# Reordering the end of the first batch's attention: the fourth pair's queries before the second pair's values, its scores and block sums before transposes back, its exponentials first on ScalarE, and the begun tiles behind the last values

## The chip, the cores and the metric

The kernel runs on one core of a Trainium2 chip. The metric is device time in microseconds (us). A profile also has a span, from the first to the last instruction that it records; it is 1.7 to 2.1 us shorter than the time of the same run. Runs that were timed in rounds were all in the fast state; a kernel that ran only once has the state "unknown", and I use such a run for its trace and not for its time.

All times inside a trace are counted from the start of its span.

## The reference, cut to what matters

```
q, k, v: 4 batches x 8 heads x 768 tokens x 64
local scores of a token: keys within 16 positions; beside them 24 summary scores,
        against the maximum of each block of 32 keys
a     = softmax(local and summary scores together)
attn  = a @ [values, block means of the values]
x     = attn as 3072 x 512
P     = exp(x @ w_gate), then 8 rounds of row and column scaling
out   = sum over 8 experts of P[:, e] * (relu(x @ w1[e]) @ w2[e])
```

The experts are most of the work. They need x, so before the first expert can stream, the first batch has to go through attention, and that start is what the change reorders.

## The kernel before

Heads are taken in pairs, four pairs to a batch, numbered from 0. The first batch is done in two halves of its tokens. For pair i and the first half, these steps run, and each has a letter in the orders below:

| letter | step | engine, line in the profile |
|---|---|---|
| T, Q | transposes of keys, of queries (PSUM) | PE, L300 and L312 |
| S, X | local scores, their exponentials | PE L347, ScalarE (ACT) L490 |
| m, s, e | key maximum of each block, summary scores, their exponentials | VectorE (DVE) L335, PE L452, ACT L472 |
| v, V | block sums of the values, their scaled copy | PE L357, DVE L363 |
| b | masks over the exponentials | DVE L495 and L500 |
| A, n | values times weights, division by the sum | PE L512, DVE L542 and L543 |
| t, x | transposes of the result, their copy to xT | PE L550, copy L207 on ACT or DVE |

The "begun tiles" are twelve single matmuls of the first expert (L211, `hps<-xT,w`), begun while attention still runs: three output tiles, each needing xT of pair 0, 1, 2 and 3 in turn.

```
def block_sums(i):                                   # v: needs the load of the pair's values
    sv = v_x[i % NQ]
    vs = bank("a", "vs")
    ...
        nc.tensor.matmul(vs..., lhsT=m_blk[:, g, :], rhs=sv[:, :, g, 0:D], ...)      # L357

def values_h(i, h):                                  # A
    ...
    av = at["av", i, h] = bank("a", "av")            # one of 3 PSUM banks
    ...

def x_out(eng, i, h=None):                           # x: frees the bank of t
    ...
    copy(eng, xT[:, i % PB, t0:t0 + n], at.pop(("tx", i, h))[:, 0:n])                # L207
```

The three banks tagged "a" are shared by v, A and t. A unit that opens a bank must wait until the unit that had that bank before was read out; which reader it waits for changes with the order, and was read from the semaphores of the built program. A planner puts all units in an order for each engine; for the first batch that order is prescribed:

```
plan.follow("PE",  "T0 F0 Q0 v0 S0 T1 Q1 s0 S1 T2 Q2 s1 A0 S2 v1 T3 A1 Q3 s2 t0 S3 v2 t1 s3 v3 A2 A3 t2 t3")
plan.follow("DVE", "m0 V0 k1 m1 b0 q2 b1 n0 V1 m2 b2 n1 m3 x1 V2 b3 V3 n2 n3 x3")
plan.follow("ACT", "k0 q0 X0 q1 e0 X1 k2 e1 X2 k3 q3 x0 e2 X3 e3 x2")
expert0(0, ...)      # begun tiles: may start once s3 is done ("U["ss", PB-1, 0]")
...
for u in plan.order():      # the list in which instructions are emitted
    u.fn()
```

(F0 in the PE order is a filler at the start and not a begun tile. The calls are shortened: the strings are split and looked up.) Loads of queries, keys and values are issued by GpSimd (POOL), one behind the other on one queue; the fourth pair's values (v3's load) are the last of the first batch.

The softmax here doesn't subtract the row's maximum and nothing guards it: scores larger than these inputs give would overflow.

## Time and profile before

| | before |
|---|---|
| time, median of 3 runs | 667.41 us (667.11 to 668.03) |
| span of the profile, granted clock | 665.94 us, 1.00 |
| TensorE busy | 99% of the span |
| fourth pair's transposes t3 start | 20.65 us |
| first instruction from which both orders are the same to the end (the "join": query transposes of the second half, L312) | 21.41 us |

This is PE's timeline before (columns: start us, duration us, engine, line, operation, output and inputs, shape, count):

```profile
15.57 0.34 PE L550 MATMUL tx<-ident_x,xs 128*128 128x128 f16 x3
15.84 0.39 PE L347 MATMUL sg<-qT,kT 64*128 64x160 bf16 x8
...
20.83 0.65 PE L211 MATMUL hps<-xT,w 128*128 128x384 f16 x3
21.41 0.38 PE L312 MATMUL tkq<-ident,qst 64*64 64x64 bf16 x12
```

The reader is to see the order t0, then S3 at 15.84, and at the other end three begun tiles at 20.83 and the join at 21.41. The join is the place at which to compare kernels: a matmul starts only after those before it, so a difference there is the net effect of everything that the change touched.

### The profile page before, as it was taken

What the parts mean: (1) busy time and instruction counts of PE and PEld (TensorE: products, weight loads), DVE (VectorE), ACT (ScalarE), POOL (GpSimd) and SP (SyncE); (2) the same over time, 40 slices, a digit from 0 to 9 for tenths busy, and PEclk for the clock granted to TensorE, in tenths of its full rate; (3) what the DMA queues carried; (4) which work ended last, traced back from release to release, by engine and by line L of the source; (5) the groups of instructions that cost most, each with busy time, mean ns of one, the idle gap of its engine ahead of it and who ended that gap; (6) DMA issues with size and microseconds to landing.
All of it is one profiled execution on the core that took longest, in us unless ns stands there. A gap on an engine that the chain in (4) does not pass through costs nothing.

```text
span 665.9 us, 13246 instructions
## 1 busy us (share of the span) xinstructions
PE 658.1 (99%) x5132; PEld 434.5 (65%) x5132; DVE 550.3 (83%) x1034; ACT 411.8 (62%) x769; POOL 199.0 (30%) x257
## 2 busy tenths in 40 slices
PE   8999999999999999999999999999999999999997
PEld 4666656555676666666666666666666666666666
DVE  7899977798989887887779877888778877988776
ACT  6677766566875566556665665555655656556652
POOL 8999522100132222212322222213122213222123
PEclk9999999999999999999999999999999999999999
DMA  9999952700763747373754666373838465334656
GB/s 168 183 148 144 136 70 42 127 0 2 134 118 62 123 75 123 66 127 65 110 97 72 119 88 104 64 127 65 127 64 138 69 95 96 64 64 111 155 135 202
DMA packets 112558, 67.89 MB, mean 102 GB/s; under 512 B 77936, under 2 KB 90480, under 8 KB 112496
## 3 DMA queue, kind: packets, MB, share of 16 engines
q0 software_dynamic: 94816, 57.46, 65.3%
q1 hardware_dynamic: 17152, 9.58, 6.2%
q8 instruction: 40, 0.66, 0.4%
q14 instruction: 22, 0.18, 0.1%
q10 hardware_dynamic: 528, 0.02, 0.0%
HBM read 52.45 MB, written 6.29 MB: 88 GB/s over the span
## 4 chain that ended last, share of the span: by engine, by line
PE 93%; DMA 3%; issue 1%; DVE 1%; POOL 0%; ACT 0%; POOLq 0%; DVEq 0%; ACTq 0%
PE yps L815 21%; PE pA L764 21%; PE pY L815 16%; PE pQ L764 10%; PE hps L211 6%; PE yps L216 6%; PE pR L764 5%; DMA out_acc<-y 2%; PE sg L347 1%; PE tkq L303 1%; DMA qst<-in_q_dram 1%; PE vs L357 1%; PE av L435 1%; PE av L512 1%; PE tx L550 1%
## 5 line engine op out<-in xcount | busy, mean ns | idle before, releaser
L815 PEld LDWEIGHTS <-h 128*128 128x128 f16 x2352 | 230.1, 98 | 89.9 <-issue 2.0
L843 POOL DMA_DIRECT2D out_acc<-y x120 | 101.4, 888 | 373.0 <-ACT y L839 107.0
L839 ACT ACTIVATE y<-pY,P_sb 128x256 f32<-128x256 f32 x168 | 80.0, 477 | 126.7 <-PE pY L815 124.0
L830 DVE SCALAR_TENSOR_TENSOR out_acc<-yps,P_sb,out_acc 128x512 f32<-128x512 f32 x128 | 95.3, 745 | 28.0 <-PE yps L815 27.9
L798 DVE TENSOR_TENSOR h<-h 128x1024 f16<-128x1024 f16 x168 | 109.2, 684 | 1.3
L815 PE MATMUL pY<-w,h 128*128 128x256 f16 x672 | 100.3, 273 | 0.6 <-ACT y L839 0.6
L764 PE MATMUL pA<-xT,w 128*128 128x512 f16 x336 | 98.6, 379 | 0.0
L815 PE MATMUL yps<-w2sum,h 128*128 128x256 f16 x672 | 97.9, 273 | 0.0
L815 PE MATMUL yps<-w,h 128*128 128x256 f16 x672 | 93.3, 273 | 0.0
L830 DVE SCALAR_TENSOR_TENSOR out_acc<-pY,P_sb,out_acc 128x512 f32<-128x512 f32 x84 | 62.9, 749 | 29.7 <-PE pY L815 28.1
L764 PEld LDWEIGHTS <-w 128*128 128x128 f16 x672 | 65.8, 98 | 31.3 <-issue 0.2
L764 PEld LDWEIGHTS <-w1sum 128*128 128x128 f16 x504 | 49.3, 98 | 44.6
L786 DVE CUSTOM_DVE_ANT_0 h<-pQ,snap 128x512 f16<-128x512 f32 x84 | 57.7, 686 | 6.5 <-ACT snap L207 3.6
L786 DVE CUSTOM_DVE_ANT_0 h<-pA,snap 128x512 f16<-128x512 f32 x84 | 57.5, 684 | 5.4 <-PE pA L764 5.0
L202 ACT ACTIVATE h<-pA 128x512 f16<-128x512 f32 x84 | 50.6, 603 | 12.1 <-PE pA L764 12.0
L202 ACT ACTIVATE h<-pR 128x512 f16<-128x512 f32 x84 | 50.1, 596 | 8.1 <-PE pR L764 8.1
L815 PE MATMUL pY<-w2sum,h 128*128 128x256 f16 x336 | 50.4, 273 | 0.6 <-ACT y L839 0.5
L207 ACT COPY pR<-pA 128x512 f32<-128x512 f32 x82 | 46.8, 571 | 6.7 <-PE pA L764 5.9
L764 PE MATMUL pA<-xsum,w 128*128 128x512 f16 x168 | 50.0, 379 | 0.0
L764 PE MATMUL pQ<-xsum,w1sum 128*128 128x512 f16 x168 | 50.0, 379 | 0.0
L764 PE MATMUL pR<-xT,w 128*128 128x512 f16 x168 | 50.0, 379 | 0.0
L764 PE MATMUL pQ<-xT,w1sum 128*128 128x512 f16 x168 | 50.0, 379 | 0.0
(150 smaller groups left out, 851.6 us busy)
## 6 DMA issues: line engine op xcount, KB each, us to landing
out_acc<-y POOLq DMA_DIRECT2D x120, 256.0 KB, 3.4
w<-in_moe_w_dram POOLq DMA_DIRECT2D x14, 1024.0 KB, 10.3
out_dram<-out_acc SPq DMA_DIRECT2D x24, 256.0 KB, 2.4
qst<-in_q_dram POOLq DMA_DIRECT2D x32, 96.0 KB, 5.6
vx<-in_v_dram POOLq DMA_DIRECT2D x15, 192.0 KB, 6.4
kst<-in_k_dram POOLq DMA_DIRECT2D x24, 96.0 KB, 5.7
w<-in_moe_w_dram POOLq DMA_DIRECT2D x4, 256.0 KB, 7.0
w<-in_moe_w_dram POOLq DMA_DIRECT2D x2, 512.0 KB, 8.5
```

What stands on the lines that cost most here:

```text
L202: nc.scalar.activation(out=out, in_=in_, func=AF.Relu, bias=0.0, scale=1.0)
L207: (nc.scalar.copy if eng == "ACT" else nc.vector.tensor_copy)(out=out, in_=in_)
L211: nc.tensor.matmul(hp[:, 0:n], lhsT=w1s[e][:, dk, f * 128:(f + 1) * 128], rhs=xT[:, dk, t0:t0 + n], start=(dk == 0), stop=(dk == KD - 1))
L216: nc.tensor.matmul(yp[:, d], lhsT=h[:, f, c * 128:(c + 1) * 128], rhs=w2s[e][:, f, d], start=(f == 0), stop=(f == KF - 1))
L303: nc.tensor.transpose(t[:, g * 128:(g + 1) * 128], st[:, g, :, :].rearrange("p j d -> p (j d)"), ident)
L764: nc.tensor.matmul(dst[:], lhsT=lhsT, rhs=rhs, start=first and k == 0, stop=k == HK - 1, skip_group_check=True)
L786: nc.vector._custom_dve(dve_ops.TENSOR_ADD_SAT, out=ring(e, p, q)[:, q % 2, blk, :], in0=at[src, e, p, q][:], in1=at.pop(("snap", n, e, p, ...
L798: nc.vector.tensor_tensor(out=h[:, :, out_, :], in0=h[:, :, a, :], in1=h[:, :, b, :], op=op)
L815: nc.tensor.matmul(dst[:, d], lhsT=lhsT, rhs=rhs, start=f == 0 and n in (1, 5, 2), stop=f == HF - 1, skip_group_check=True)
L830: nc.vector.scalar_tensor_tensor(out=o, in0=y, scalar=scalar, in1=o, op0=ALU.mult, op1=ALU.add)
L839: nc.scalar.activation(out=at[key][:, d], in_=src, func=AF.Copy, bias=0.0, scale=P_sb[:, t, e:e + 1])
L843: nc.gpsimd.dma_start(out=o, in_=at.pop(("y", e, p, c, key))[:], accum_op=ALU.add)
```

## The change

Its intent is to get the fourth pair's exponentials and masks done earlier, so that the last two values groups follow each other at once, and to let the begun tiles fill the wait behind them. It moves Q3 before A1, S3 before t0 and v3 before t1 on PE; it puts X3 first on ScalarE, with e2 ahead of x0 behind it, and gives the copy x1 from VectorE to ScalarE; and the begun tiles wait for A3.

```diff
-  m = add("PE", 0.165, ..., [xs[dk], w[f // 2], m if dk else U["ss", PB - 1, 0]], ...)
+  m = add("PE", 0.165, ..., [xs[dk], w[f // 2], m if dk else U["A", PB - 1, 0]], ...)
 ...
-  "T0 F0 Q0 v0 S0 T1 Q1 s0 S1 T2 Q2 s1 A0 S2 v1 T3 A1 Q3 s2 t0 S3 v2 t1 s3 v3 A2 A3 t2 t3"     # PE
+  "T0 F0 Q0 v0 S0 T1 Q1 s0 S1 T2 Q2 s1 A0 S2 v1 T3 Q3 A1 s2 S3 t0 v2 v3 t1 s3 A2 A3 t2 t3"
-  "m0 V0 k1 m1 b0 q2 b1 n0 V1 m2 b2 n1 m3 x1 V2 b3 V3 n2 n3 x3"                                # DVE
+  "m0 V0 k1 m1 b0 q2 b1 n0 V1 m2 b2 n1 m3 V2 b3 V3 n2 n3 x3"
-  "k0 q0 X0 q1 e0 X1 k2 e1 X2 k3 q3 x0 e2 X3 e3 x2"                                            # ACT
+  "k0 q0 X0 q1 e0 X1 k2 e1 X2 k3 q3 X3 e2 x0 e3 x1 x2"
```

More of the change, by code (lines that the diff above doesn't have):

```diff
@@ L1000, in expert0 @@
                         m = add("PE", 0.165, lambda f=f, dk=dk: hidden0(key, t0, f, [dk]),
-                                [xs[dk], w[f // 2], m if dk else U["ss", PB - 1, 0]], 9 + f * 0.01,
+                                [xs[dk], w[f // 2], m if dk else U["A", PB - 1, 0]], 9 + f * 0.01,
                                 **{"uses" if dk else "opens": [buf]})
@@ L1075 @@
         plan.follow("PE", [first[c[0]](int(c[1])) for c in
-                           "T0 F0 Q0 v0 S0 T1 Q1 s0 S1 T2 Q2 s1 A0 S2 v1 T3 A1 Q3 s2 t0 S3 v2 t1 s3 v3 A2 A3 t2 t3".split()])
+                           "T0 F0 Q0 v0 S0 T1 Q1 s0 S1 T2 Q2 s1 A0 S2 v1 T3 Q3 A1 s2 S3 t0 v2 v3 t1 s3 A2 A3 t2 t3".split()])
         plan.follow("DVE", [first[c[0]](int(c[1])) for c in
-                            "m0 V0 k1 m1 b0 q2 b1 n0 V1 m2 b2 n1 m3 x1 V2 b3 V3 n2 n3 x3".split()])
+                            "m0 V0 k1 m1 b0 q2 b1 n0 V1 m2 b2 n1 m3 V2 b3 V3 n2 n3 x3".split()])
         plan.follow("ACT", [first[c[0]](int(c[1])) for c in
-                            "k0 q0 X0 q1 e0 X1 k2 e1 X2 k3 q3 x0 e2 X3 e3 x2".split()])
+                            "k0 q0 X0 q1 e0 X1 k2 e1 X2 k3 q3 X3 e2 x0 e3 x1 x2".split()])
         expert0(0, [U["x", i, 0] for i in range(PB)])
```

## The prediction

> **What bounds the kernel now.** I read the page first: the busy row, and the summary of the chain that ended last.
>
> ```profile
> PE 658.1 (99%) x5132; PEld 434.5 (65%) x5132; DVE 550.3 (83%) x1034; ACT 411.8 (62%) x769; POOL 199.0 (30%) x257
> ...
> PE 93%; DMA 3%; issue 1%; DVE 1%; POOL 0%; ACT 0%; POOLq 0%; DVEq 0%; ACTq 0%
> ```
>
> TensorE carries 93% of the chain and its clock row shows full speed in every slice. The instruction order of the two builds gives 10,242 rows on PE in both and no difference after about 21 us: the change adds no work and removes none, it reorders a stretch between 13 and 21 us. So only the empty places of PE in that stretch can be gained. I looked for them next, in PE's timeline (columns: start us, duration us, engine, line, operation). Since the ends are modelled, I take start to next start as what a group occupies.
>
> ```profile
> 16.17 0.52 PE L357 MATMUL vs<-vx,m_blk 128*128 128x128 bf16 x6
> 16.52 0.33 PE L550 MATMUL tx<-ident_x,xs 128*128 128x128 f16 x3
> 16.91 0.34 PE L452 MATMUL ss<-qT,ks 64*32 64x384 bf16 x2
> 17.18 0.52 PE L357 MATMUL vs<-vx,m_blk 128*128 128x128 bf16 x6
> ...
> 18.36 0.66 PE L211 MATMUL hps<-xT,w 128*128 128x384 f16 x3
> 18.86 0.63 PE L512 MATMUL av<-vx,Eh 128*128 128x65 bf16 x16
> ...
> 20.04 0.49 PE L211 MATMUL hps<-xT,w 128*128 128x384 f16 x2
> 20.65 0.34 PE L550 MATMUL tx<-ident_x,xs 128*128 128x128 f16 x3
> ```
>
> Three tx transposes occupy 0.17 us where nothing waits (19.87 to 20.04), but those at 16.52 last until 16.91: 0.22 us empty. Two hps matmuls occupy 0.33 (three take 0.50 at 18.36), but those at 20.04 last until 20.65: 0.28 us empty. The weight loads name the causes:
>
> ```profile
> 16.91 0.09 PEld L452 LDWEIGHTS <-ks 64*32 64x32 bf16 x2 [0.23 <-DVE ks L335]
> ...
> 20.64 0.17 PEld L550 LDWEIGHTS <-xs 128*128 128x128 f16 x3 [0.51 <-DVE xs L543]
> ```
>
> The first waits for the fourth pair's key maximum, the second for the fourth pair's normalized values. Together 0.50 us, 0.07% of 667.41: that is nearly all the change can win here, and no state or clock effect is in play.
>
> **What the Trainium skill says.** "TensorE: Matmul & The Clock Gate", section "The mechanism", says matmuls start and end in strict program order. That is why one late operand holds all behind it; the trace agrees (nothing between 16.69 and 16.91 though other operands were ready). "Perfetto Trace Analysis", section "Tensor Engine Instruction (MATMUL, LD_WEIGHTS)", says the matmul end is an estimate; the trace agrees, groups overlap on paper (16.17 + 0.52 is after 16.52). "ScalarE: Activation LUTs", section "What ACT_TABLE_LOAD costs", gives 186 ns + 0.833 ns per column with immediates, and 93 ns of overlap back to back: 1.01 us for 992 columns, 0.51 for 384. The trace has 0.98 and 0.48, and a spacing of 0.87 and 0.39; I use the trace's.
>
> **The change, part by part.** Letters: Q queries' transposes, S scores, X their exponentials, s/e summaries and their exponentials, v/V block sums and their copy, A values, n normalize, t/x transposes back and their copy, F the begun hidden tiles; the pair's number from 0.
>
> *Q3 ahead of A1.* Twelve transposes of 0.31 us (14.67 to 14.98) swap with A1's 0.84 (13.83 to 14.67). The sum is the same, so s2 still starts at 15.30. Q3's copy on ScalarE can start after the key copy, 14.74, and end near 15.14: in time for S3.
>
> *S3 ahead of t0, X3 first on ScalarE.* S3 starts behind s2 at 15.57 instead of 15.84, its last matmul ends at 15.96. X3 was held by two others:
>
> ```profile
> 15.95 0.48 ACT L207 COPY xT<-tx 128x384 f16<-128x384 f16 x1 [0.38 <-PE tx L550]
> 16.32 0.48 ACT L472 ACTIVATE es<-ss 64x384 bf16<-64x384 f32 x1
> 16.71 0.98 ACT L490 ACTIVATE erh<-sg 128x992 bf16<-128x992 f32 x1
> ```
>
> Now X3 runs 16.01 to 17.00, 0.70 earlier. The price: e2 starts at 16.88 and x0 at 17.27, ending 17.75 instead of 16.43.
>
> *Masks and values.* VectorE does:
>
> ```profile
> 15.91 0.94 DVE L335 TENSOR_REDUCE ks<-kT 128x24 bf16<-128x768 bf16 x1
> 16.89 0.36 DVE L207 COPY xT<-tx 128x384 f16<-128x384 f16 x1
> 17.16 0.28 DVE L363 TENSOR_TENSOR Vs<-vs,own_n 64x128 bf16<-64x128 f32 x1
> 17.72 0.66 DVE L495 TENSOR_TENSOR Eh<-erh,band 128x960 bf16<-128x960 bf16 x1 [0.28 <-ACT erh L490]
> ```
>
> The copy x1 goes to ScalarE, so V2 moves to 16.78-17.06 and the masks of pair 3 to about 17.04-17.77, 0.68 earlier (they ended at 18.45). A3 may then follow A2 directly, without the three F between.
>
> *New waits.* I read from the build which semaphore each PE instruction waits for. v3 now stands before t1, and needs its load and n1 (done 16.00). t1's PSUM slot is v2's, so it waits for V2: 17.06 + 0.04 = 17.10. A2's slot is t0's, so it waits for x0: 17.79. For v3's load I have the queue that waits for its landing:
>
> ```profile
> 16.89 0.75 POOL L190 DMA_DIRECT2D w<-in_moe_w_dram  x1 [1.16 <-DMA vx<-in_v_dram]
> ```
>
> The fourth pair's values landed shortly before 16.89 (the trace's own record: 16.61). So v3 can't start at 16.41, where PE would be ready, but at 16.66 to 16.9.
>
> *The sum.* Occupancies from the timeline: S 0.32, t 0.17 (0.27 before a 64-row group), v 0.35, s 0.27, A 0.84, F 0.165 each. S3 15.57-15.89, t0 to 16.06, v2 to 16.41, **wait 0.25**, v3 16.66-17.01, **wait 0.09**, t1 17.10-17.37, s3 to 17.64, **wait 0.15**, A2 17.79-18.63, A3 to 19.47, two F to 19.80, t2 to 19.97, four F to 20.62, t3 at 20.62. n3 needs A3's end + 0.10 + 0.79 + 0.06 = 20.42, so t3 no longer waits for it: the six F (the same six as before, all ahead of t3) fill that gap. Before, t3 started at 20.65. The two waits of 0.50 us go; three of 0.49 come. **Net gain: 0.03 us**, and about 0.1 at most if v3's load arrives as recorded. Behind t3 both orders are the same, so what is left at t3 stays to the end. PE waits for no load between 21 and 110 us in the view of waits, so an earlier or later PE is not absorbed.
>
> **The rivals.**
> 1. *The intended gain.* A3 ends at 19.45 instead of 19.70, all F fill the wait for n3; if PE did not wait for v3's load and x0, t3 could start 0.3 to 0.45 earlier: 667.0. For it: X3 and the masks really come 0.7 earlier. Against it: the landing at 16.61 and x0 at 17.75 are the new ends of the waits. If ScalarE gets through e2 sooner (it can't start before X3 ends), or the load lands earlier in that run, up to 0.2 of this is won.
> 2. *The wait grows.* v3 stands ahead of t1, s3 and both A in strict order, so a later landing delays them one for one once it exceeds about 16.8. The loads between 5 and 20 us run on DMA engines that are busy in every slice (9 tenths), so a landing moves from run to run; 0.3 later makes 667.6.
> 3. *VectorE or DMA takes the shift back later.* VectorE is busy 7.8 to 9 tenths there, but the loads of the second batch land 2 us and more before PE uses them (the fifth pair's keys by 25.05, used at 27.87), so I see no absorber; this would only pull the result towards 667.4.
>
> **Range and chances.** 667.41 less 0.03, and a little for rival 1, which I hold more likely than rival 2 (the order was written to shorten this stretch): 667.3 us. The three runs before span 667.11 to 668.03, 0.9 us, far more than the effect; a new median of few runs should differ by 0.3 or 0.4 by itself. Add 0.3 for the mechanism: 666.6 to 668.0 holds 8 in 10. A 2% step is 13.3 us, 26 times all the idle time in the stretch: same 0.98, faster 0.01, slower 0.01.
>
> **What would show each step right or wrong.** In the changed profile: S3 at 15.5 to 15.6 and the exponential of 992 columns right behind, near 16.0; the fourth pair's vs group later than the end of the third's, waiting for a vx load or starting at 16.6 to 16.9; the first values after s3 near 17.8, with ScalarE's xT copy ending just before; the two values groups back to back; no wait of a tx weight load for xs near 20.6; the tx of the fourth pair at 20.4 to 20.8. Busy time of all engines unchanged. The prediction is wrong if the tx of the fourth pair starts before 20.2 or after 21.0, or if PE shows a new gap behind 21 us, which I exclude because the order there is the same; and a difference beyond 1 us between fast runs would need a cause that I do not see.

## The result, and the profile after

| | before | after |
|---|---|---|
| median of 5 runs | 667.38 us (667.11 to 668.03) | 667.65 us (667.14 to 668.09) |
| span of the profile | 665.94 us | 665.93 us |
| t3 starts | 20.65 us | 20.96 us |
| join | 21.41 us | 21.71 us |

The ratio is 1.0003, with a 95% interval of 0.9990 to 1.0017: the same. (A ratio is the mean time of one kernel's runs over the mean of the other's in the same rounds, so it is not quite the ratio of the medians.) The busy row and the summary of the chain say nearly the same as before (POOL has the 1% that VectorE had):

```profile
PE 658.9 (99%) x5132; PEld 434.9 (65%) x5132; DVE 550.2 (83%) x1033; ACT 411.7 (62%) x770; POOL 198.8 (30%) x257
...
PE 93%; DMA 3%; POOL 1%; issue 1%; ACT 0%; DVE 0%; POOLq 0%; DVEq 0%; ACTq 0%
```

One instruction has gone from VectorE to ScalarE (1034 to 1033 and 769 to 770: the copy x1), and nothing else was added or removed. This is PE's timeline in the stretch, after:

```profile
15.56 0.39 PE L347 MATMUL sg<-qT,kT 64*128 64x160 bf16 x8
...
16.07 0.51 PE L357 MATMUL vs<-vx,m_blk 128*128 128x128 bf16 x6
17.25 0.50 PE L357 MATMUL vs<-vx,m_blk 128*128 128x128 bf16 x6 [0.68 <-DMA vx<-in_v_dram]
17.59 0.33 PE L550 MATMUL tx<-ident_x,xs 128*128 128x128 f16 x3
...
18.12 0.64 PE L512 MATMUL av<-vx,Eh 128*128 128x65 bf16 x16
...
18.96 0.64 PE L512 MATMUL av<-vx,Eh 128*128 128x65 bf16 x16
...
20.96 0.33 PE L550 MATMUL tx<-ident_x,xs 128*128 128x128 f16 x3
```

The fourth pair's scores are first, at 15.56. The third pair's block sums start at 16.07 and occupy 0.34 us, so PE was ready for the fourth pair's at 16.41. It started them at 17.25. The bracket gives the idle time and its releaser: 0.68 us, until the load of vx landed. (0.68 is counted from the modelled end of the group before; from the next possible start it is 0.84.) From there on nothing waits. The two values groups follow each other (18.12, 18.96), and t3 comes at 20.96.

ScalarE, VectorE and GpSimd in that order show the rest, after:

```profile
16.06 1.00 ACT L490 ACTIVATE erh<-sg 128x992 bf16<-128x992 f32 x1 [0.95 <-ACT qT L207]
...
17.32 0.47 ACT L207 COPY xT<-tx 128x384 f16<-128x384 f16 x1
```

```profile
17.09 0.66 DVE L495 TENSOR_TENSOR Eh<-erh,band 128x960 bf16<-128x960 bf16 x1
```

```profile
17.40 0.74 POOL L190 DMA_DIRECT2D w<-in_moe_w_dram  x1 [1.23 <-DMA vx<-in_v_dram]
```

The exponentials start at 16.06 and the masks at 17.09, where the prediction had 16.01 and 17.04. So the wanted effect came, 0.63 to 0.65 us earlier than before. The copy x0 ends at 17.79. GpSimd, which waits for the same load as PE, is released at 17.40, where it was 16.89 before. The trace's own record has the load landed at 17.11, against 16.61 before.

Two questions follow. Is the late landing the whole of the 0.30 us at the join? And did the new order cause it? A third is why the two profiles have the same span although one is 0.30 us behind at the join.

### The profile page after: what moved, and what is told of

Its sections match the earlier page's. It is cut to its first block, busy times and chain, and to the rows that moved or that the text cites. A ratio compares the mean times of both kernels' runs of the same rounds, so it can differ in the third digit from the quotient of the medians.

```text
span 665.9 us, 13247 instructions
## 1 busy us (share of the span) xinstructions
PE 658.9 (99%) x5132; PEld 434.9 (65%) x5132; DVE 550.2 (83%) x1033; ACT 411.7 (62%) x770; POOL 198.8 (30%) x257
## 4 chain that ended last, share of the span: by engine, by line
PE 93%; DMA 3%; POOL 1%; issue 1%; ACT 0%; DVE 0%; POOLq 0%; DVEq 0%; ACTq 0%
PE yps L815 21%; PE pA L764 21%; PE pY L815 16%; PE pQ L764 10%; PE hps L211 6%; PE yps L216 6%; PE pR L764 5%; DMA out_acc<-y 2%; PE sg L347 1%; DMA vx<-in_v_dram 1%; PE tkq L303 1%; PE vs L357 1%; PE av L512 1%; PE av L435 1%; PE tx L550 1%
## 5 line engine op out<-in xcount | busy, mean ns | idle before, releaser
L764 PE MATMUL pA<-xsum,w1sum 128*128 128x512 f16 x168 | 50.0, 379 | 0.0
```

Source lines behind the costliest of these rows:

```text
L764: nc.tensor.matmul(dst[:], lhsT=lhsT, rhs=rhs, start=first and k == 0, stop=k == HK - 1, skip_group_check=True)
```

## The experiments

**Theory A.** The landing moves from run to run for reasons that are not in the order; the new order exposes it, and the landing at 17.11 is the whole loss. With an early landing, the changed kernel is where the one before is. **Rival B.** Something else, x0 and the bank that it frees or the place of the begun tiles, holds t3 near 20.96 anyway. **Rival C.** The new order makes the load land later. (The expectation of a_again gives the letter C to another rival, that t3 lies anywhere by scatter; t3 3.71 us behind v3 in both late runs speaks against that one.) There was also a constructive question: which parts of the change are worth keeping?

Instead of prescribing another order to the planner, I moved single units in the finished list, which leaves everything behind the join as it was. All edits below use this helper, ahead of the emission, and the data dependencies are asserted again:

```
seq = plan.order()
def behind(after, *us):
    for u in us:
        seq.remove(u); seq.insert(seq.index(after) + 1, u); after = u
...                                                  # the edit of the experiment
assert all(at_[d] < at_[u] for u in seq for d in u.true)
```

### Summary of the traces

Landing is the trace's own record of v3's load. The last column counts from the start of s2 (15.28 to 15.45 in all of them), which removes small shifts that were there before the stretch.

| run | order | v3's load landed | v3 starts | A2 | A3 | t3 | join | join behind s2 |
|---|---|---|---|---|---|---|---|---|
| before | before | 16.61 | 17.18 | 17.53 | 18.86 | 20.65 | 21.41 | 6.11 |
| b_again | before | 16.79 | 17.21 | 17.57 | 18.90 | 20.69 | 21.45 | 6.12 |
| b_look2 | before | 16.52 | 17.25 | 17.61 | 18.94 | 20.73 | 21.49 | 6.11 |
| b_look3 | before | 16.63 | 17.22 | 17.57 | 18.91 | 20.70 | 21.45 | 6.11 |
| after | changed | 17.11 | 17.25 | 18.12 | 18.96 | 20.96 | 21.71 | 6.42 |
| a_again | changed | 17.34 | 17.48 | 18.35 | 19.19 | 21.19 | 21.94 | 6.64 |
| a_look2 | changed | 16.56 | 16.70 | 18.00 | 18.83 | 20.83 | 21.58 | 6.13 |
| a_look3 | changed | 16.59 | 16.72 | 17.84 | 18.67 | 20.67 | 21.41 | 6.12 |
| v3_other | changed, v3 reads another load | 17.04 | 16.41 | 17.84 | 18.67 | 20.67 | 21.42 | 6.12 |
| v3_back | changed, v3 behind s3 | 16.59 | 17.21 | 17.88 | 18.71 | 20.71 | 21.46 | 6.12 |
| best | changed, v3 behind A2 | 17.04 | 18.01 | 17.16 | 18.37 | 20.43 | 21.18 | 5.89 |
| F_late | before, begun tiles behind A3 | 16.76 | 17.16 | 17.52 | 18.42 | 20.42 | 21.41 | 6.12 |
| F_early | changed, begun tiles before A3 | 17.33 | 17.47 | 18.34 | 19.73 | 21.51 | 22.27 | 6.99 |
| x_act | changed, X3 third on ScalarE | 16.42 | 16.55 | 17.42 | 18.89 | 20.87 | 21.62 | 6.24 |

### The changed kernel again: a_again, a_look2, a_look3

All three are the changed kernel unaltered.

> The changed kernel unaltered. Theory A (TensorE waits in strict order for the fourth pair's value load, whose landing moves by some tenths from run to run): its block sums start 0.1 us behind the landing, wherever that is between 16.6 and 17.3 us, and the fourth pair's transposes back (t3) start 3.7 us later: 20.6 if the load lands by 16.6, 20.96 if at 17.1. Rival B (the late copy x0 on ScalarE and the PSUM slot behind it set the second wait): t3 at 20.96 wherever the load lands. Rival C (nothing but scatter): t3 anywhere. Time 667.3 to 667.9.

> Changed kernel, another look (17.11 and 17.34 so far). Scatter: anywhere from 16.4 to 17.35, and t3 3.71 behind the start of the block sums unless they start before 16.75, when V2 and x0 take over and t3 is at 20.65. Changed order delays the load: 17.0 to 17.4 in both looks.

> A third look at the changed kernel beside it: 16.4 to 17.35 if it is scatter, 17.0 to 17.4 if the changed order delays the load; t3 3.71 behind the start of the block sums, or at 20.65 with an early load.

a_again took 667.62 us (667.41 to 667.87, 6 runs), 0.9994 of the kernel before in the same rounds (0.9981 to 1.0007; before 667.74). Its profile has the load even later, at 17.34, and a wait to match. a_look2 and a_look3 (one run each, 667.35 and 667.00) have it at 16.56 and 16.59. Here is PE in a_look3:

```profile
16.72 0.51 PE L357 MATMUL vs<-vx,m_blk 128*128 128x128 bf16 x6 [0.15 <-DMA vx<-in_v_dram]
17.09 0.33 PE L550 MATMUL tx<-ident_x,xs 128*128 128x128 f16 x3
...
17.84 0.63 PE L512 MATMUL av<-vx,Eh 128*128 128x65 bf16 x16
...
20.67 0.33 PE L550 MATMUL tx<-ident_x,xs 128*128 128x128 f16 x3
```

and one line of a_look2, whose stretch runs 0.16 us later throughout:

```profile
18.00 0.63 PE L512 MATMUL av<-vx,Eh 128*128 128x65 bf16 x16 [0.23 <-ACT xT L207]
```

With an early load, the wait at v3 shrinks to 0.15 us, and a wait for ScalarE's copy x0 at A2 takes its place, as the prediction had it. The join is 6.12 and 6.13 us behind s2, against 6.11 before. So the changed order with an early load is no faster than the order before, and with a late one it is slower.

The size follows too. Behind v3 come 0.34, 0.26 and 0.27 us of PE work up to A2, and A2 can't start before 17.84. So a v3 that starts by 16.97 costs nothing, that is, a load that lands by about 16.84 (v3 started 0.13 to 0.14 us after the recorded landing in all four runs). The scored profile was 0.27 beyond that and A2 0.28 later than 17.84; a_again was 0.50 beyond and A2 0.51 later. Theory A holds in size.

### The kernel before again: b_again, b_look2, b_look3

> The kernel before unaltered, to see where the fourth pair's value load lands in another of its runs and what that does. A: block sums start at 17.18 if the load lands by 17.0, else 0.1 behind the landing; t3 at 20.65 or later by the excess. Rival (the changed kernel makes the load land later): here it lands at 16.6 again, and later only in the changed order. Span 665.3 to 665.9.

> Kernel before, another look at where the fourth pair's value load lands (16.61 and 16.79 so far). If landing is scatter of the run: anywhere from 16.4 to 17.35. If the changed order delays it: 16.6 to 16.8 in both looks at this kernel. Either way block sums at 17.2 or 0.13 behind the landing, t3 3.48 behind their start.

> A third look at the kernel before, for the scatter of the landing: 16.4 to 17.35 if it is scatter, 16.6 to 16.8 if the changed order delays it; t3 3.48 behind the start of the block sums.

One run each: 667.27, 667.17 and 667.13 us. The load landed between 16.52 and 16.79 and v3 never waited for it, because PE reaches it only near 17.2. The join is 6.11 or 6.12 us behind s2 each time: the yardstick is good to 0.01 us.

### Taking the load away: v3_other and v3_back

```diff
 # v3_other, on the changed kernel
-    sv = v_x[i % NQ]
+    sv = v_x[1 if i == 3 else i % NQ]        # block sums of the second pair's values: wrong on purpose

 # v3_back, on the changed kernel
+    behind(U["ss", 3, 0], U["vs", 3])        # v3 back to its old place, behind s3
```

> The changed kernel, its fourth block sums reading the second pair's values, which landed long ago: wrong result on purpose, the wait for the load gone, all else the same. A: block sums at 16.4, next wait for V2 (t1 at 17.1), next for x0 (A2 at 17.8), t3 at 20.6 to 20.7, 0.3 earlier than in the changed kernel; time 0.3 us less, 667.35. B: t3 stays at 20.96, time unchanged.

> The changed kernel, with the fourth block sums put back behind s3 as before, everything else in the changed order. A: t1 at 16.4, s3 at 16.9 (waits for the key maximum), block sums at 17.16 or at the landing, A2 at 17.8 (waits for x0), t3 at 20.65; time 0.3 less than the changed kernel, 667.35. B: t3 stays at 20.96.

v3_other gives a wrong result on purpose (relative error 0.335), as it sums values that landed long before. In its profile the load was late, at 17.04, but no longer waited for by v3, which started at 16.41. Its PE timeline:

```profile
17.84 0.63 PE L512 MATMUL av<-vx,Eh 128*128 128x65 bf16 x16
...
20.67 0.33 PE L550 MATMUL tx<-ident_x,xs 128*128 128x128 f16 x3
```

and that of v3_back, which is correct:

```profile
17.88 0.63 PE L512 MATMUL av<-vx,Eh 128*128 128x65 bf16 x16
...
20.71 0.33 PE L550 MATMUL tx<-ident_x,xs 128*128 128x128 f16 x3
```

Two different ways of hiding the load give the same t3, near 20.7. Rival B, which needed 20.96, falls. But neither gains on the kernel before: x0, which ends on ScalarE at 17.79 and 17.83, then holds A2 at 17.84 and 17.88. The waits for the load and for x0 lie one behind the other, and taking away the first only uncovers the second. Times: 667.66 us (667.05 to 668.66) and 668.08 (667.33 to 668.68), ratios 0.9995 (0.9981 to 1.0008) and 1.0000 (0.9986 to 1.0014), 6 runs each: no difference that these can tell, so the times forecast for them, 0.3 us less, are neither confirmed nor refuted.

### The begun tiles alone: F_late and F_early

```diff
 # F_late, on the kernel before: three begun tiles from before A3 to behind it
+    behind(U["A", 3, 0], U["F", 0, 0], U["F", 0, 1], U["F", 1, 0])

 # F_early, on the changed kernel: back to before A3, behind x1
+    behind(U["x", 1, 0], U["F", 0, 0], U["F", 0, 1], U["F", 1, 0])
```

> The kernel before, with only the third part of the change: the three begun tiles that stood between the last two values groups go behind the second of them. A and my sum: A3 starts at 18.4 (its masks end then) instead of 18.86, n3 ends near 20.2, the six F fill until 20.42, t3 at 20.4 with no wait: 0.23 ahead of before. If the masks or the fourth block sums' copy hold A3, t3 at 20.6. Time 667.2.

> The changed kernel without its third part: three begun tiles go back between the last two values groups. A: A3 0.5 to 0.55 later, n3 with it, and t3 waits for it some 0.3 us: t3 4.05 behind the start of the fourth block sums, against 3.71 in both runs of the changed kernel. If the begun tiles did not matter, 3.71.

F_late (667.35 us, 667.17 to 668.66, 6 runs; ratio 0.9995, 0.9977 to 1.0014) moved t3 to 20.42, 0.23 us ahead of the kernel before. And yet its join is at 21.41, 6.12 behind s2 as ever. PE and then ScalarE tell why:

```profile
20.42 0.33 PE L550 MATMUL tx<-ident_x,xs 128*128 128x128 f16 x3
20.83 0.65 PE L211 MATMUL hps<-xT,w 128*128 128x384 f16 x3
```

```profile
20.30 0.48 ACT L207 COPY xT<-tx 128x384 f16<-128x384 f16 x1 [2.25 <-PE tx L550]
```

The begun tiles behind t3 multiply xT of the third pair, and ScalarE's copy x2 ends at 20.78. They start at 20.83, exactly as in the kernel before. The gain at t3 was real and was given back at the next group, to a wait that t3 had covered until then. My forecast, which followed t3 alone, missed this. t2 had not moved forward (19.93, against 19.87 before); x2 and what waits for it follow t2.

F_early (one run, 667.98 us, late load at 17.33) does the reverse. Its PE timeline has the three tiles between the values groups:

```profile
17.47 0.51 PE L357 MATMUL vs<-vx,m_blk 128*128 128x128 bf16 x6 [0.91 <-DMA vx<-in_v_dram]
...
19.18 0.71 PE L211 MATMUL hps<-xT,w 128*128 128x384 f16 x3
```

t3 comes at 21.51, 4.04 us behind v3, as forecast (4.05), where the changed kernel has 3.71. Within the changed order and with a late load, the third part of the change is worth 0.33 us at t3, and as much at the join (4.80 us behind v3, against 4.46 in a_again). With an early load it was not run.

### The exponentials alone: x_act

```diff
 # on the changed kernel: ScalarE does x0 and e2 first again, then X3
+    behind(U["vs", 2], U["x", 0, 0], U["sx", 2, 0], U["X", 3, 0])
```

> The changed kernel with ScalarE's order taken back (x0, e2, then the fourth pair's exponentials X3), so these start near 17.0 instead of 16.06. A: the wait for the load has hidden all that X3 first gained, A3 starts right behind A2 all the same: t3 3.71 behind the start of the fourth block sums, as in the changed kernel. If the early exponentials count, t3 4.0 or more behind it.

The forecast, t3 3.71 us behind v3, was missed: it was 4.32, since the load came at 16.42, the earliest of all (one run, 667.41 us). This doesn't decide for the alternative of "4.0 or more" either, because the changed kernel itself has 3.95 and 4.13 with an early load; the join behind s2 has to decide. With an early load the masks are what A3 waits for:

```profile
18.89 0.63 PE L512 MATMUL av<-vx,Eh 128*128 128x65 bf16 x16 [0.55 <-DVE Eh L500]
```

A2 started at 17.42, since x0 was early again, and A3 waited 0.55 us. The join is 6.24 behind s2, against 6.12 in the changed kernel with an early load. So ScalarE's new order as a whole, with X3 early and x0 late, is worth 0.12 us when the load is early. With a late one, the masks (done at 18.86 here) would be done before A3 could start anyway (18.96 in the scored profile), so they would be worth nothing; that is argued, not run.

### A version from what was learnt: best

```diff
 # on the changed kernel
+    behind(U["A", 2, 0], U["vs", 3])         # v3 behind A2: off the load
+    behind(U["x", 1, 0], U["sx", 3, 0])      # x1 ahead of e3 on ScalarE
```

> Fourth block sums behind the third pair's values A2, and the second pair's copy x1 ahead of e3 on ScalarE. Both the load and x0 then have 0.9 us more. A and my sum: t1 16.4, s3 16.9, A2 17.16, block sums 18.0, A3 18.35, t3 at 20.35: 0.3 ahead of the kernel before, 0.6 ahead of the changed one; time 667.05. If another wait takes over (x1 for the slot of A3), t3 at 20.5 to 20.7.

Only A3 needs v3's sums, so v3 can stand behind A2. With v3 no longer ahead of it, A2 gets another bank and doesn't wait for x0: it started at 17.16, while x0 ran on ScalarE from 17.31 on. PE in best:

```profile
17.16 0.64 PE L512 MATMUL av<-vx,Eh 128*128 128x65 bf16 x16
...
18.01 0.52 PE L357 MATMUL vs<-vx,m_blk 128*128 128x128 bf16 x6
18.37 0.63 PE L512 MATMUL av<-vx,Eh 128*128 128x65 bf16 x16
...
20.43 0.33 PE L550 MATMUL tx<-ident_x,xs 128*128 128x128 f16 x3
20.60 0.65 PE L211 MATMUL hps<-xT,w 128*128 128x384 f16 x3
```

The load landed late in this run too, at 17.04, and cost nothing. t3 came at 20.43 (forecast 20.35; 0.07 of the difference is a wait of t2 for n2, which ended at 19.55), and unlike in F_late the tiles behind it follow at once, because t2 moved forward as well, to 19.60. The join is 5.89 behind s2: 0.22 us ahead of the kernel before, and 0.53 ahead of the scored run of the changed one. In this stretch best beats both, by one profile of it. The two moves of best were not run apart. In time that can't be shown: 667.77 us (666.99 to 668.86, 6 runs), against 667.74 (667.27 to 670.47, 11 runs), ratio 1.0000 with an interval of 0.9984 to 1.0016. The interval is plus or minus 1.07 us, five times the effect.

### The span: a second wait, far from the change

The 0.30 us at the join stay in the trace for more than 500 us, and then go at once. These are the same matmul in the profile before and in the one after:

```profile
554.97 0.60 PE L815 MATMUL pY<-w2sum,h 128*128 128x256 f16 x4 [0.48 <-ACT y L839]
```

```profile
554.97 0.60 PE L815 MATMUL pY<-w2sum,h 128*128 128x256 f16 x4 [0.18 <-ACT y L839]
```

Both wait for a ScalarE instruction, and both start at 554.97: the wait ends at the same moment in both, and the run that is 0.30 us ahead waits 0.30 longer. Two instructions back stands a transfer. In the profile before, ScalarE waited 1.25 us for an accumulating transfer to land (out_acc<-y), and in both profiles an earlier such transfer, issued right behind a 1 MB weight load, took 12.2 us; the median of that stretch is 4.3. GpSimd could issue the next one only when that had landed, at 551.02 in both. In the profile after, ScalarE's releaser is named otherwise (a PE group that had ended by then), but the trace's own record has the transfer issued at 551.02 land at 554.36 in both, 0.08 us before ScalarE went on. b_look3 has the earlier transfer at 10.6 us, no wait, and the matmul at 554.36.

The other runs bear this out. From the join to the end of the span it is 643.87 to 643.94 us in eleven of the 14 profiles, of both orders, and more in three: 644.53 before, 644.22 after, and 644.12 in v3_other, where ScalarE waited 0.84 us for the same transfer. In these three the earlier transfer took 12.1 to 12.2 us, in the others 10.5 to 11.9. So apart from this transfer, what stands at the join arrives at the end: the spans are 665.05 in best, 665.29 to 665.37 in the three repeats of before and in a_look3, and 665.88 in a_again. That the two scored profiles have the same span is chance, as both had the late transfer.

### What stays open

Rival C is not fully excluded. Over all 14 profiles the load landed between 16.42 and 17.34. Beyond 16.84 it was in 5 of the 9 kernels built on the changed order and in none of the 5 built on the old one. If lateness had nothing to do with the order, all five would fall among the nine with a probability of 126/2002, 6%. Against a cause in the order speaks that the same changed kernel landed at 16.56, 16.59, 17.11 and 17.34, and that in the scored profile the second pair's load was already late (5.9 us from issue to landing, against 5.0 before), before the two orders part at 13.8 us. But v3_back had 5.8 there, and then the fourth pair's load landed early, at 16.59. Nor did the changed order put other transfers ahead of the load: between 13.8 and 16.4 us only GpSimd's queue moved data, in all 14 profiles. The count is also mixed with the chip, which the record names for all but the two scored profiles. The four on chip 6 all had the changed order, and three of them were late. On chips 12 and 14, where both orders ran, none of four with the old order was late and one of four with the new one. What moves the landing was not found; that the DMA engines are busy, as the prediction has it, was not tested as its cause.

Also open is whether best is faster in time. And one cheap rival order was not tried: x0 straight behind X3, ahead of e2, would let x0 end about 0.37 us earlier (an estimate, from e2's start at 16.95 to x0's at 17.32), and so perhaps take away the wait for it at A2.

## Why the prediction was right or wrong

It said 667.3 us (666.6 to 668.0) and "same"; 667.65 came. The class and the range were right, and the mechanism mostly so. The time itself tests little of the mechanism: the scatter of the runs, 0.9 us, is larger than everything that either rival would have done, and the two scored profiles have equal spans by chance. The traces test it. The sum, term by term, against the two kinds of run:

| start of | predicted | early load (a_look3) | scored (after) |
|---|---|---|---|
| S3 | 15.57 | 15.56 | 15.56 |
| v2 | 16.06 | 16.06 | 16.07 |
| v3 | 16.66 | 16.72 | **17.25** |
| t1 | 17.10 | 17.09 | 17.59 |
| A2 | 17.79 | 17.84 | 18.12 |
| A3 | 18.63 | 18.67 | 18.96 |
| t3 | 20.62 | 20.67 | 20.96 |

- **Bound and size.** TensorE's order bounds this stretch and there was only half a microsecond to win: right. Nothing in any run moved the join forward by more than 0.23 us.
- **Q3, S3, X3 and masks.** Right to within 0.05 us.
- **The new waits.** All three exist. With an early load, they come where the prediction put them and eat the gain, as the middle column shows. In the scored run the first had swallowed the other two. One reading in that sum is loose: the 0.22 us "empty" behind t1 takes its length as 0.17, where the sum itself has 0.27 ahead of a 64-row group. So about 0.12 of it was waiting. The other 0.10 comes back in the changed order because t0 no longer stands ahead of such a group. The total stays.
- **The term that was mis-sized** is "wait 0.25" in front of v3. It measured 0.84 us, since the load landed at 17.11. I had taken 16.61, the landing of one trace, as a property of the kernel, and let v3 start by 16.9 at the latest. It scatters over 0.9 us. Of the 0.34 us by which t3 missed the sum, 0.28 are this, and 0.05 are small errors that the early run has too.
- **The wrong choice between rivals** is "rival 1, which I hold more likely than rival 2". Rival 2, the landing that "delays them one for one once it exceeds about 16.8", is what happened, and 16.8 was a good threshold (16.84 by the sum above). I shifted the centre down by 0.1 us for rival 1; in the scored run the loss went the other way.
- **"What is left at t3 stays to the end"** was a step too short. It holds where t3 moves back. F_late shows that a t3 0.23 us earlier gains nothing while x2 isn't earlier too. So the stated gain of 0.03 us at t3 didn't have to arrive at the join in any case.
- **"A new gap behind 21 us, which I exclude"**: the gap after, of 0.18 us at 554.97, is not new, since the profile before has 0.48 there. But I had checked the waits only to 110 us, and so "an earlier or later PE is not absorbed" was wrong for these two profiles: this gap absorbed the whole 0.30.
- **Its own signs.** t3 was to come at 20.4 to 20.8 and came at 20.96, so that sign failed. Its limit for being wrong, t3 after 21.0, was not reached in the scored profile, but a_again, the same kernel with a later landing, has t3 at 21.19. Which side of the limit the scored profile fell on was luck.
- **ScalarE.** The prediction's 1.01 and 0.51 us are estimates, worked out from the formula that it cites. It used the trace's 0.98 and 0.48 instead, and X3 took 1.00 in the profile after.
- **The range** was rightly drawn from the scatter of the runs, which is several times larger than anything in the stretch.

## What to carry to other kernels

Before moving a consumer forward in a strict order, ask for the landing of its load in several traces and not in one: this one moved by 0.9 us, and the order before had a slack of 0.3 to 0.6 us (v3's start less the landing, less 0.13) that nobody saw because nothing waited. Move forward what needs only what is long there, and put the consumer of the latest load directly ahead of the one that needs it, as best does. And follow a gain past the instruction at which it shows: F_late's 0.23 us were gone at the next group, in a wait that had been hidden behind the one removed.

## What the Trainium skill lacked or had wrong

- "DMA: Bandwidth & Descriptors", section "🔬 Anatomy of one DMA — SWDGE (gpsimd) path", gives one cost for one transfer, about 2.0 us + bytes / 436e3 per us. For the 192 KB that the profile counts for a load of values, I estimate from it 2.5 us. The three such loads of the first batch, issued behind others on the same queue, took 5.0 to 7.9 us from issue to landing in the 14 profiles. The section has no figure for what waiting behind other loads adds, nor for the scatter: the same load of the same program landed anywhere from 16.56 to 17.34 us.
- The same section has no figure for the step from the update of a load's semaphore, which is what the trace records as the landing, to the start of the engine that waits for it. PE started 0.13 to 0.14 us after the recorded landing. GpSimd, which waits for the same load, went on 0.28 to 0.29 us after it (16.89 against 16.61, and 17.40 against 17.11).
- The formula of the same section gives an estimate of 2.6 us for the accumulating transfers of 256 KB. Issued right behind a 1 MB weight load, one of them took 10.5 to 12.2 us, depending on the run (median of the stretch 4.3). In the profile before, PE lost about 0.65 us to it (644.53 from the join to the end, against 643.88). The section has no such case.
- "TensorE: Matmul & The Clock Gate", section "The mechanism", on the strict order of matmuls, held in every run: the late v3 delayed ready work behind it one for one. Nothing is to be mended there.
